# Moving the next batch's scores, transposes and values one product away from the bursts of packed weights

## The chip, the core and the metric

One NeuronCore of a Trainium2 chip runs the whole program. The metric is device time in microseconds, the median of several executions, lower is better. The matrix engine is called TensorE (PE in the profile, its weight loads PEld), the others are VectorE (DVE), ScalarE (ACT), GpSimd (POOL) and SyncE (SP), whose queue issues most of the DMA transfers.

## What is computed

The program has three parts, one behind the other. The attention and the first expert layer are where the change lies.

```python
def sm_attn(qq, kk, vv):
    s = scale * np.matmul(qq, kk.transpose(0, 1, 3, 2))
    s = s - np.max(s, axis=-1, keepdims=True)
    a = np.exp(s)
    a = a / (np.sum(a, axis=-1, keepdims=True) + 1e-09)
    return np.matmul(a, vv)
p_packed = sm_attn(p, k, v)           # p: 32 rows a head
out = sm_attn(q, p_packed, p_packed)  # batch 8, heads 8, seq 576, head_dim 64
...
h = np.maximum(np.maximum(x @ w1, x @ w2), x @ w3)   # 512 -> 768
x = h @ w_out                                        # 768 -> 512
...
h = x @ w_in                                         # 512 -> 2048
g = np.maximum(h, 0.0) + np.log1p(np.exp(-np.abs(h)))
return g @ w_out
```

## The kernel before

The work goes batch by batch through attention and the first expert layer, and the result of each batch goes to DRAM (x2d). When all eight batches are done, the softplus layer runs over all tokens (layer3 and layer4, lines 735 to 783); the change does not touch it.

For one batch, attention is packed onto the four heads' 32 rows. `transpose_kq` (185) turns a raw load of q or k into vT with a VectorE transpose (220 for q, 223 for k); four of each make a batch. There is one vT buffer: k's is given back by the first scores, and q's is given back by the second. `prep_p` (236) transposes p. `attn1_scores` (256) makes the first scores (matmuls at 247, 32 of them) into two PSUM tiles, and `attn1_exp` reduces them on VectorE (262) and exponentiates them on ScalarE (271). `attn1_transpose` (281, matmuls at 286) transposes the result, `attn1_values` (299, matmuls at 306) multiplies it by v, and `packed_transpose` (324) turns the 32 packed rows. `attn2_scores` (327), `attn2_weights` (345) and `attn2_split` (359) do the second attention, whose weights a2 have a high and a low part.

The second attention's values are never formed. Instead `packed_weights` (365) multiplies the packed rows into the weights w1, w2, w3, four column blocks at a time: 16 matmuls on 64*32 pieces of the array (line 375), here called a burst. The PSUM tile ps_w of a burst is emptied by two pairs of ScalarE and VectorE instructions one after the other, pwhi (107) then pwlo (108) for each half. `layer1_unit` (398) is one product: 12 matmuls of 128x288 (line 396), whose tile is emptied by a copy on ScalarE (419, the first of three) or a running maximum on VectorE (421, the other two). `layer1_split` and `layer2` (435) make the second product of the expert layer.

All of these PSUM tiles come from one pool `mm` of four buffers of two banks each, the whole PSUM.

The loop of lines 635 to 640 and behind runs over batches n = 1 to 7, and within one over ten slots: six slots of three layer1 products and four slots of layer2. The products are counted by u = 0 to 21: u = 3 * slot + w in the first six slots, u = 12 + slot behind. Before each product, `small_work(n, u)` (578) issues what belongs there: a burst of packed weights at u = 1, 5, 9 and 13, and, for the next batch m = n + 1, the pieces of its attention. `pinned` (569) ties each call's TensorE instructions behind those of the call before it, so that TensorE's order is exactly the written one. VectorE, ScalarE and the queues have no such order: a planner lays their instructions out in the order in which it expects them to become ready, and hands out the pool buffers in the same way. After each slot the lists `turns` and `loads` say which raw loads of q or k are transposed and issued; an entry (slot, ahead, g, which) means piece g of batch n + ahead. Raw loads have five buffers, and `narrow_ahead` (622) works the weights of the last layer from 64 to 32 bits in what is left of ScalarE and VectorE.

Of the kernel before, what the change touches and what calls it, by code (L numbers as in the profile page):

```python
# [19 lines left out]
def packed_attention_maxout_softplus(  # L20
# [155 lines left out]
    def load_p(n):  # L176
        t = tp.tile([P, NG, D], F32, tag="praw", name="praw")
        for G in range(NG):
            nc.sync.dma_start(
                out=t[:, G],  # L180
                in_=bass.AP(p.tensor, p[n, G].offset, [[NG * NP * D, NH], [D, NP], [1, D]]),
            )
        praw[n] = t
# [161 lines left out]
    def attn2_weights(n, G):  # L345
        s = s2.pop((n, G))
        sg = tp.tile([P, T], F32, tag="sg2", name="sg2")
        nc.vector.tensor_reduce(out=sg, in_=s, axis=AX.X, op=ALU.add)
        nc.vector.tensor_scalar(out=sg, in0=sg, scalar1=1e-9, scalar2=None, op0=ALU.add)
        rc = tp.tile([P, T], F32, tag="rc2", name="rc2")  # L350
        nc.vector.reciprocal(out=rc, in_=sg)
        nc.vector.tensor_tensor(
            out=s, in0=s, in1=rc.unsqueeze(2).to_broadcast([P, T, 32]), op=ALU.mult
        )
        a = sp.tile([P, S], F32, tag="s2", name="a2")
        nc.vector.transpose(out=a, in_=s.rearrange("p t n -> p (t n)"))
        a2[n, G] = a

    def attn2_split(n, G):
        hi = a2p.tile([P, S], F32R, tag="a2hi", name="a2hi")  # L360
        lo = a2p.tile([P, S], F32R, tag="a2lo", name="a2lo")
        split(a2.pop((n, G)), hi, lo)
        a2hi[n, G], a2lo[n, G] = hi, lo
# [176 lines left out]
    for name in order.split():  # L540
# [11 lines left out]
        (7, 2, 3, "k"),  # L552
    ]
    turns = [
        (1, 1, 0, "q"),
        (2, 1, 1, "q"),
        (3, 1, 2, "q"),
        (4, 1, 3, "q"),
        (9, 2, 0, "k"),
        (9, 2, 1, "k"),  # L560
# [8 lines left out]
    def pinned(fn, *args):  # L569

        if chain:
            with tc.issue_after(chain[-1]):
                fn(*args)
        else:
            fn(*args)
        chain.append(last_of(mybir.EngineType.PE))

    def small_work(n, u):


        m = n + 1
        more = m < B
        if u == 2 and more:
            pinned(prep_p, m)
            if m + 1 < B:
                load_p(m + 1)
        if u in (1, 5, 9, 13):
            pinned(packed_weights, n, (u + 3) // 4)
        if not more:
            return  # L590
        if u == 5:
            pinned(attn1_scores, m)
        elif u == 9:
            for G in range(NG):
                pinned(attn1_transpose, m, G)
        elif u == 13:
            pinned(attn1_values, m)
        elif u == 16:
            pinned(packed_transpose, m)
        elif u == 18:  # L600
            pinned(attn2_scores, m)
            pinned(packed_weights, m, 0)
        elif u == 20:
            for G in range(NG):
                attn2_weights(m, G)
        elif u == 21:
            for G in range(NG):
                attn2_split(m, G)
# [26 lines left out]
    for n in range(1, B):  # L635
        for slot in range(F1 + KC):
# [4 lines left out]
            if slot < F1:  # L641
                if slot == 1 and n + 1 < B:
                    load_v(n + 1)
                for w in range(3):
                    small_work(n, 3 * slot + w)
                    pinned(layer1_unit, n, slot, w)
            else:
                small_work(n, 2 * F1 + slot)
                pinned(layer2, n, slot - F1)
# [214 lines left out]
```

## Time and profile before

| | |
|---|---|
| median of 3 runs | 1338.73 us (1338.31 to 1339.14) |
| the profiled execution's own time | 1341.63 us |
| its span, first to last instruction | 1339.8 us |
| TensorE busy | 1304.5 us (97%) |
| VectorE busy | 894.2 us (67%) |
| ScalarE busy | 617.9 us (46%) |
| mean granted TensorE clock | 0.993 of full speed |

The profile is of one execution. A timeline lists instructions of one engine in order of time, equal neighbours merged; matmuls are pipelined, so the time of a group is best read from its start to the start of the next. The first batch that the loop touches is n = 1, from 128.6 us; n = 2 begins at 187.8, n = 3 at 247.0, n = 7 (which has no next batch) at 484.6, and the softplus layer at 536.9.

### The profile page before, as it was taken

The page shows a single profiled execution, that of the slowest core. Times are in us where ns is not written, and L with a number is a line of the kernel's source. Part 1 is how long each engine was busy: PE and PEld are TensorE (multiplying, and loading weights), DVE is VectorE, ACT ScalarE, POOL GpSimd, SP SyncE. Part 2 cuts the span into 40 slices and gives each one's busy share as a digit, 9 for nine tenths or more (in the row PEclk, how much of TensorE's full clock was granted, in tenths as well). Part 3 has the DMA queues.
Part 4 walks back from the last instruction along what each step waited for, and adds up shares of the span by engine and source line. Part 5 has one row for each costly group of instructions (what it writes and reads, how often), then busy time and mean ns, then how long its engine had stood idle before and what let it go on. Part 6 is the DMA issues. An engine that isn't in the chain of part 4 may idle for free.

```text
span 1339.8 us, 21462 instructions
## 1 busy us (share of the span) xinstructions
PE 1304.5 (97%) x8656; PEld 1100.2 (82%) x8656; DVE 894.2 (67%) x1480; ACT 617.9 (46%) x1045; POOL 0.7 (0%) x6
## 2 busy tenths in 40 slices
PE   4889999999999999999999999999999999999998
PEld 3778888898989899788888888888888888888887
DVE  4787778786878746866556566565665665655654
ACT  3544434444443435745445454454444544544443
POOL 0000000000000000000000000000000000000000
PEclk9979999999999999999999999999999999999999
DMA  9873677877577506501102011010020110000101
GB/s 269 214 197 92 170 202 180 208 212 204 178 201 201 134 36 215 159 0 38 26 1 64 0 32 32 0 47 17 4 60 0 32 32 0 24 8 1 32 1 32
DMA packets 61859, 119.17 MB, mean 89 GB/s; under 512 B 11072, under 2 KB 28736, under 8 KB 61760
## 3 DMA queue, kind: packets, MB, share of 16 engines
q1 hardware_dynamic: 55984, 106.66, 29.8%
q10 hardware_dynamic: 5776, 11.14, 2.5%
q8 instruction: 68, 1.11, 0.3%
q14 instruction: 31, 0.25, 0.1%
HBM read 90.51 MB, written 27.26 MB: 88 GB/s over the span
## 4 chain that ended last, share of the span: by engine, by line
PE 89%; DMA 5%; DVE 3%; ACT 1%; issue 1%; SPq 0%; DVEq 0%; ACTq 0%
PE ps L396 55%; PE acc L781 10%; PE acc L780 10%; PE acc L779 10%; PE ps_w L375 2%; DMA wraw<-in_moe_w_dram 1%; DMA wi_x<-wi 1%; PE ps_s L247 1%; PE ps_v L306 1%; PE ps_e L286 1%; DMA x2d<-xs 1%; DMA kraw<-in_k_dram 1%; DMA vt<-in_v_dram 1%; PE ps_k L199 1%; DVE pwlo L108 0%
## 5 line engine op out<-in xcount | busy, mean ns | idle before, releaser
L396 PE MATMUL ps<-x2hi,wilo 128*128 128x512 f32 x576 | 228.0, 396 | 0.0
L396 PE MATMUL ps<-x2lo,wihi 128*128 128x512 f32 x576 | 227.0, 394 | 0.0
L396 PE MATMUL ps<-x2hi,wihi 128*128 128x512 f32 x576 | 226.7, 394 | 0.0
L781 PE MATMUL acc<-w2hi,glo 128*128 128x512 f32 x576 | 226.0, 392 | 0.0
L780 PE MATMUL acc<-w2lo,ghi 128*128 128x512 f32 x576 | 225.7, 392 | 0.0
L779 PE MATMUL acc<-w2hi,ghi 128*128 128x512 f32 x576 | 224.5, 390 | 0.7 <-ACT ghi L107 0.7
L107 ACT ACTIVATE ghi<-t 128x512 fp32r<-128x512 f32 x144 | 91.0, 632 | 289.0 <-DVE t L761 288.6
L754 DVE TENSOR_SCALAR t<-ex 128x512 f32<-128x512 f32 x144 | 61.4, 426 | 161.9 <-ACT ex L751 161.9
L108 DVE TENSOR_TENSOR glo<-t,ghi 128x512 fp32r<-128x512 f32 x144 | 99.7, 692 | 92.6 <-ACT ghi L107 92.5
L396 PE MATMUL ps<-a2hi,pwhi 128*128 128x288 f32 x576 | 129.3, 307 | 2.5 <-ACT a2hi L107 1.3
L779 PEld LDWEIGHTS acc<-w2hi,ghi 128*128 128x128 f32 x576 | 108.2, 188 | 25.8 <-ACT ghi L107 1.2
L396 PEld LDWEIGHTS ps<-x2lo,wihi 128*128 128x128 f32 x576 | 108.1, 188 | 25.8
L396 PEld LDWEIGHTS ps<-x2hi,wilo 128*128 128x128 f32 x576 | 108.3, 188 | 25.2
L750 ACT ACTIVATE ex<-ps 128x512 f32<-128x512 f32 x144 | 86.2, 598 | 92.3 <-PE ps L396 92.2
L780 PEld LDWEIGHTS acc<-w2lo,ghi 128*128 128x128 f32 x576 | 108.1, 188 | 25.0
L396 PEld LDWEIGHTS ps<-x2hi,wihi 128*128 128x128 f32 x576 | 108.1, 188 | 24.5
L781 PEld LDWEIGHTS acc<-w2hi,glo 128*128 128x128 f32 x576 | 108.1, 188 | 23.5 <-DVE glo L108 0.4
L396 PE MATMUL ps<-a2lo,pwhi 128*128 128x288 f32 x576 | 124.3, 298 | 0.7 <-DVE a2lo L108 0.7
L396 PE MATMUL ps<-a2hi,pwlo 128*128 128x288 f32 x576 | 124.2, 297 | 0.0
L757 DVE TENSOR_TENSOR t<-ln,t 128x512 f32<-128x512 f32 x144 | 99.7, 692 | 30.4 <-ACT ln L752 30.4
L396 PEld LDWEIGHTS ps<-a2hi,pwhi 128*128 128x128 f32 x576 | 93.1, 192 | 15.8 <-ACT m L419 5.9
L761 DVE SCALAR_TENSOR_TENSOR t<-ps,t 128x512 f32<-128x512 f32 x144 | 99.5, 691 | 4.7
(90 smaller groups left out, 1847.9 us busy)
## 6 DMA issues: line engine op xcount, KB each, us to landing
qraw<-in_q_dram SPq DMA_DIRECT2D x112, 140.0 KB
kraw<-in_k_dram SPq DMA_DIRECT2D x96, 140.0 KB
wraw<-in_moe_w_dram SPq DMA_DIRECT2D x18, 512.0 KB
x2d<-xs ACTq DMA_DIRECT2D x32, 288.0 KB
x2r<-x2d SPq DMA_DIRECT2D x36, 256.0 KB
out_dram<-o SPq DMA_DIRECT2D x136, 64.0 KB
raw<-in_moe_w_in_dram SPq DMA_DIRECT2D x16, 512.0 KB
raw<-in_moe_w_out_dram SPq DMA_DIRECT2D x16, 512.0 KB
```

The source lines that it names most:

```text
L107: nc.scalar.activation(out=hi, in_=src, func=AF.Copy)
L108: nc.vector.tensor_tensor(out=lo, in0=src, in1=hi.bitcast(F32), op=ALU.subtract)
L199: nc.tensor.matmul(ps[64 * G : 64 * G + 64, i // hi, c : c + rows], r[:, i, G], ident[:rows, :rows], start=True, stop=True,)
L375: nc.tensor.matmul(ps[cols, G, : units * P].rearrange("p (w x) -> p w x", w=units), ppT[n][rows, cols], wsb[rows, 4 * c : 4 * c + units, g ...
L396: nc.tensor.matmul(o, w, xx, start=first, stop=last)
L750: nc.scalar.activation(out=ex, in_=ps, func=AF.Abs)
L754: nc.vector.tensor_scalar(out=t, in0=ex, scalar1=1.0, scalar2=-1.0, op0=ALU.add, op1=ALU.add)
L757: nc.vector.tensor_tensor(out=t, in0=ln, in1=t, op=ALU.subtract)
L761: nc.vector.scalar_tensor_tensor(out=t, in0=ps, scalar=0.0, in1=t, op0=ALU.max, op1=ALU.add)
L779: nc.tensor.matmul(ps, ghi[:, cols], whi, start=(f == 0), stop=False)
L780: nc.tensor.matmul(ps, ghi[:, cols], wlo, start=False, stop=False)
L781: nc.tensor.matmul(ps, glo[:, cols], whi, start=False, stop=(f == F2 - 1))
```

## The change

The first scores of the next batch go from u = 5 to u = 6, the transposes from u = 9 to u = 10, the values from u = 13 to u = 14. So one layer1 product stands between each of them and the burst of packed weights that they followed directly. The first three transposes of q each go one slot further down, because the single vT buffer is not free before the first scores have run.

```diff
     turns = [
-        (1, 1, 0, "q"),
-        (2, 1, 1, "q"),
-        (3, 1, 2, "q"),
+        (2, 1, 0, "q"),
+        (3, 1, 1, "q"),
+        (4, 1, 2, "q"),
         (4, 1, 3, "q"),
...
         if not more:
             return
-        if u == 5:
+        if u == 6:
             pinned(attn1_scores, m)
-        elif u == 9:
+        elif u == 10:
             for G in range(NG):
                 pinned(attn1_transpose, m, G)
-        elif u == 13:
+        elif u == 14:
             pinned(attn1_values, m)
         elif u == 16:
             pinned(packed_transpose, m)
```

## Rows read from the trace of the kernel before

**Rows 1.** The chain that ended last, by engine (section 4 of the page).

```profile
PE 89%; DMA 5%; DVE 3%; ACT 1%; issue 1%; SPq 0%; DVEq 0%; ACTq 0%
```

**Rows 2.** Busy times by stretch, batches n = 2 and n = 3.

```profile
core 0: us, PE busy (x) PEld busy (x) DVE busy (x) ACT busy (x) POOL busy (x), PEclk, DMA share, GB/s
187.80:247.00 59.20, 58.88 (x616) 53.05 (x615) 46.27 (x81) 25.04 (x44) 0.00 (x0) 1.00 0.76 196
247.00:306.40 59.40, 59.09 (x616) 53.10 (x615) 47.15 (x83) 25.00 (x44) 0.00 (x0) 1.00 0.75 201
```

**Rows 3.** Timeline of TensorE, batch n = 7: a burst alone (start us, us, engine, line, operation).

```profile
484.57 0.43 PE L396 MATMUL ps<-a2hi,pwhi 128*128 128x288 f32 x2
...
486.26 1.09 PE L375 MATMUL ps_w<-wsb,ppT 64*32 64x512 f32 x16
487.28 0.53 PE L396 MATMUL ps<-a2hi,pwhi 128*128 128x288 f32 x2
...
488.96 0.43 PE L396 MATMUL ps<-a2hi,pwhi 128*128 128x288 f32 x2
...
490.56 0.43 PE L396 MATMUL ps<-a2hi,pwhi 128*128 128x288 f32 x2
```

**Rows 4.** Timeline of TensorE, n = 2, u = 5 to 8.

```profile
197.22 1.09 PE L375 MATMUL ps_w<-wsb,ppT 64*32 64x512 f32 x16
198.10 1.18 PE L247 MATMUL ps_s<-vT,pT 64*32 64x288 f32 x32
199.21 0.53 PE L396 MATMUL ps<-a2hi,pwhi 128*128 128x288 f32 x2
...
201.24 0.51 PE L396 MATMUL ps<-a2hi,pwhi 128*128 128x288 f32 x2 [0.18 <-DVE pwlo L108]
...
203.20 0.53 PE L396 MATMUL ps<-a2hi,pwhi 128*128 128x288 f32 x2
...
204.90 0.43 PE L396 MATMUL ps<-a2hi,pwhi 128*128 128x288 f32 x2
```

**Rows 5.** Timeline of VectorE, n = 2: the second pwlo.

```profile
200.40 0.69 DVE L108 TENSOR_TENSOR pwlo<-ps_w,pwhi 128x512 fp32r<-128x512 f32 x1 [0.66 <-ACT pwhi L107]
```

**Rows 6.** Timeline of TensorE, n = 3, the first scores and the product behind.

```profile
257.30 0.68 PE L247 MATMUL ps_s<-vT,pT 64*32 64x288 f32 x12
258.29 1.16 PE L247 MATMUL ps_s<-vT,pT 64*32 64x288 f32 x20 [0.31 <-DVE vT L223]
259.38 0.53 PE L396 MATMUL ps<-a2hi,pwhi 128*128 128x288 f32 x2
```

**Rows 7.** Timeline of VectorE, n = 3: maximum of u = 4, last k transpose.

```profile
256.60 0.76 DVE L421 TENSOR_TENSOR m<-ps,m 128x576 f32<-128x576 f32 x1 [0.89 <-PE ps L396]
257.27 0.97 DVE L223 STREAM_TRANSPOSE vT<-kraw 128x576 f32<-128x576 f32 x1
```

**Rows 8.** Timeline of TensorE: half-size burst before values (n = 3), before a product (n = 7).

```profile
274.81 0.66 PE L375 MATMUL ps_w<-wsb,ppT 64*32 64x256 f32 x16
275.40 1.55 PE L306 MATMUL ps_v<-vt,e1T 96*32 96x64 f32 x96
...
509.04 0.66 PE L375 MATMUL ps_w<-wsb,ppT 64*32 64x256 f32 x16
509.63 0.53 PE L396 MATMUL ps<-a2hi,pwhi 128*128 128x288 f32 x2
```

**Rows 9.** Timeline of TensorE, first stretch: transposes of e behind a product.

```profile
64.80 0.43 PE L396 MATMUL ps<-a2hi,pwlo 128*128 128x288 f32 x2
65.07 0.82 PE L286 MATMUL ps_e<-ident,e 128*96 128x128 f32 x6
```

**Rows 10.** Timelines, n = 3: the last q transpose, the second scores.

```profile
281.57 0.77 DVE L220 STREAM_TRANSPOSE vT<-qraw 128x576 f32<-128x576 f32 x1
285.15 1.20 PE L247 MATMUL ps_s<-vT,ppT 64*32 64x288 f32 x32
```

**Rows 11.** Timeline of VectorE: first k transpose of a batch, ahead of n = 3 and n = 4.

```profile
236.24 0.97 DVE L223 STREAM_TRANSPOSE vT<-kraw 128x576 f32<-128x576 f32 x1
...
295.62 0.96 DVE L223 STREAM_TRANSPOSE vT<-kraw 128x576 f32<-128x576 f32 x1
```

## The prediction

> **What bounds the kernel now.** I read the chain of waits first. TensorE holds 89% of the chain that ended last, so the time is TensorE's, and any other engine counts only where TensorE waits for it [rows 1]. Then the busy times by stretch: the second of the batches that the change touches (n = 2) takes 59.20 us and the third (n = 3) 59.40, of which TensorE is busy 58.88 and 59.09, at the full 2.4 GHz (granted clock 1.00) [rows 2]. So there is very little idle time, and the question is what TensorE does product by product. I therefore read the timeline of TensorE and took the distance from the start of one product to the start of the next. The reader should see three things in it.
>
> A first-layer product with nothing special beside it takes 1.60 us (488.96 to 490.56). A burst of packed weights by itself costs 1.02 us, and it also lengthens its neighbours: the product before it takes 1.69 and the one behind it 1.68 [rows 3]. So entering and leaving a burst costs about 0.09 and 0.08.
>
> At u = 5 the packed weights and the first scores stand back to back. In n = 2 the burst goes over to the scores after 0.88 us and the scores to the product behind them after 1.11. But the next three products take 2.03, 1.96 and 1.70 (199.21 to 201.24, to 203.20, to 204.90). The first of these delays is put down to the second pwlo, which ends at 201.09 [rows 4, 5]. It is what gives back the PSUM buffer of the packed weights: there are four, and the two scores tiles take two at once.
>
> In n = 3 the same place looks different. The products behind are ordinary, but the scores take 2.08 us in place of 1.11, cut in two by a wait for the last transpose of k [rows 6]. That transpose starts at 257.27, right behind the maximum of u = 4, without any wait for a transfer beside it [rows 7]. So it is late by its place in VectorE's order, not by its load. The batches n = 4, 5 and 6 repeat n = 3 (scores of 2.08 each), and n = 1 repeats n = 2.
>
> **What the change takes away.** Six batches have a next one (n = 1 to 6). In n = 1 and 2 the excess is (2.03 - 1.69) + (1.96 - 1.60) + (1.70 - 1.60) = 0.80 us. With one product between burst and scores, the scores ask for their two buffers one product later, and that product, with a border on either side, takes 1.60 + 0.09 + 0.08 = 1.77 us. The product behind the scores then starts 1.02 + 1.77 + 1.11 = 3.90 us after the burst began. By then the buffer of u = 5 is free, since the maximum that empties it is 0.76 us long [rows 7] and has 1.11 us for it. In n = 3 to 6 the excess is 2.08 - 1.11 = 0.97. The scores now start at 257.30 - 0.88 + 1.02 + 1.77 = 259.2, a microsecond after the transpose of k ends (257.27 + 0.97), so that wait is gone. Sum: 2 x 0.80 + 4 x 0.97 = 5.48 us.
>
> **What it adds.** No instruction is new; what is added are the borders of the bursts.
> - Scores at u = 6: burst and scores no longer overlap (1.02 against 0.88: 0.14) and there is one more way in and out (0.09 + 0.08). 0.31.
> - Values at u = 14: one more way in and out. The half-size burst goes over to the values after 0.59 us, and to a product in the last batch after the same 0.59, so standing next to a burst saves the values nothing on their way in [rows 8]. 0.17.
> - Transposes at u = 10: in the first stretch of the kernel they follow a product at its ordinary distance (0.27 for two matmuls, 64.80 to 65.07) [rows 9], so only the way out of the burst is new, 0.08 at most, less what the transposes now lose at their own start. Between 0.03 and 0.08; I take 0.06.
>
> Together 0.54 us in each of six batches, 3.24 us.
>
> **What is moved and covered.** The q transposes (0.77 us each, two now in one slot) go to VectorE beside products. The last of them starts at 281.57 in n = 3 and the second scores, which need it, at 285.15 [rows 10]. One more in front of it leaves 3.58 - 0.77 - 0.77 = 2.04 us; without that cover, a delay would pass to TensorE one for one. The loads keep their slots on SP's queue; a raw buffer comes free up to 5 us later, far ahead of the k load that takes it. The values come 1.7 us nearer to the transpose of their result at u = 16: two products (3.3 us) are left for two short VectorE operations. I cost these at nothing. What is late next is the buffer of the packed weights at u = 6 and u = 10, by a margin of some 0.2 us or less. It costs nothing if the planner hands out the buffer of the product between, and some 0.6 us a batch at u = 6 if not (rival B).
>
> **The sum.** 5.48 - 3.24 = 2.24 us less. The profiled execution took 1341.63 us, 2.90 above the median of the runs (1338.73), so 1339.4 for it and 1336.5 for the median. Below, 0.2% (2.7 us) is about what a measurement of this kernel can tell from no change.
>
> A page speaks against part of this sum. The Trainium skill, "TensorEngine Tiling (Array Packing)", section Key Properties, says that going over to another tiling mode, not just another tile, drains TensorE. It prices no drain.
>
> **Rivals.**
> A, borders are counted by changes of shape. Packed weights and scores share 64*32, the values are 96*32, and the transposes pass as whole. Then the scores add two changes, the values one (from burst to values is one already) and the transposes none: three more of (0.09 + 0.08) / 2 = 0.085, plus 0.14. That is 0.40 us a batch, 2.4 in all, 3.1 us less: 1335.6. This is how the page's rule would count. For it: the transposes show no drain [rows 9]. Against it: the 0.59 on both sides [rows 8]. Chance 0.20.
>
> B, the PSUM wait stays. If the maximum of u = 5 is put ahead of the second pwlo and the planner hands u = 6 the packed weights' buffer, the maximum ends 1.02 + 1.77 + 0.76 = 3.55 us after the burst began, the pwlo 0.69 later, and the product goes 0.15 after that (201.09 to 201.24): 4.4 against 3.90. With the 0.10 that a broken product costs, that is 0.6 us in six batches, 3.6 less the 2.24: 1.4 us slower, 1340.1. For it: the four buffers are as full as before at that place. Against it: the buffer of u = 5 is free first. Chance 0.15.
>
> C, slower: the last transpose of k slides along with the scores. Its place on VectorE is set by the planner, and if that puts it behind the maximum of u = 5 in n = 3 to 6, it starts near 260.05 (259.2, 0.08 for the end of the product, 0.76) and ends at 261.0. The product behind the scores starts 1.14 us after it as now (258.24 to 259.38), at 262.1 against 259.2 + 1.11 = 260.3: a wait of 1.8 us in place of 0.97. Four batches lose 1.8 + 0.54 - 0.97 = 1.37 each, two gain 0.26: 5.0 us slower, 1343.7. It decides from a wait of 0.56 us (no gain left) and shows as slower from 1.23. Against it: the first k transpose of a batch stands 10.8 us ahead of the next batch's start both before n = 3 and before n = 4 (236.24, 295.62), though n = 2 had no such wait and n = 3 had [rows 11]; so the order of the k transposes is tied to the products and does not drift. Chance 0.12.
>
> That the change does not do what it says is hardly open: TensorE's order is pinned step by step. VectorE's is not, and that is C.
>
> **How the numbers follow.** My forecast (the waits go, the borders cost 0.54) has 0.53, with 1336.0 to 1337.4 as its own range; A has 0.20, B 0.15, C 0.12. The range from 1335.2 to 1340.2 takes in A and B, and leaves out C and the edges. Faster by over 0.2% means below 1336.05: A, and a twentieth from the edge of the forecast, 0.25. Slower means above 1341.4: C and a little of B, 0.14. The rest, 0.61, lies within 0.2%.
>
> **What would show it.** In the changed profile n = 2 and n = 3 should both take about 58.95 us. The scores should stand between two ordinary products with about 1.11 to the next start, without a bracket that names the k transpose; the product between burst and scores should take 1.77. The transposes of e should follow a product with no gap. A unit of 2 us behind the scores would be B, and scores of 2 us or more C. If the product between bursts takes 1.69, it is A. I am wrong altogether if a new wait stands at u = 10, 14 or 16.

## The result, and the profile after

The changed kernel took 1346.06 us (median of 4 runs, 1344.45 to 1349.45) against 1338.93 for the kernel before (4 runs): a ratio of 1.0055, with a 95% interval from 1.0042 to 1.0067. It is 7.1 us slower. I had forecast 1336.5, with at most 1340.2.

First the busy times of the changed kernel by stretch, batches n = 2 and n = 3, which answer to [rows 2].

```profile
184.10:243.35 59.25, 59.22 (x616) 52.93 (x615) 45.57 (x81) 25.16 (x44) 0.00 (x0) 1.00 0.75 192
243.35:304.33 60.98, 59.88 (x616) 53.02 (x615) 46.99 (x83) 24.86 (x44) 0.00 (x0) 1.00 0.72 196
```

Both should have taken 58.95. Batch n = 2 takes 59.25, and n = 3 takes 60.98 where it took 59.40 before. TensorE is busy for only 59.88 of it, at the full clock (1.00), so the batch contains a wait.

The timeline of TensorE in n = 2, around u = 5 and 6, answers to [rows 4] and shows the intended part of the change.

```profile
193.48 1.09 PE L375 MATMUL ps_w<-wsb,ppT 64*32 64x512 f32 x16
194.50 0.52 PE L396 MATMUL ps<-a2hi,pwhi 128*128 128x288 f32 x2
...
196.27 1.20 PE L247 MATMUL ps_s<-vT,pT 64*32 64x288 f32 x32
197.40 0.53 PE L396 MATMUL ps<-a2hi,pwhi 128*128 128x288 f32 x2
...
199.09 0.42 PE L396 MATMUL ps<-a2hi,pwhi 128*128 128x288 f32 x2
```

From start to start the burst takes 1.02, the product between 1.77 (194.50 to 196.27), the scores 1.13, and the next product 1.69. The delays of 2.03 and 1.96 behind the scores are gone. All of that is as forecast.

The same place in n = 3 on TensorE, to set beside [rows 6]:

```profile
255.52 0.70 PE L247 MATMUL ps_s<-vT,pT 64*32 64x288 f32 x12
257.30 1.16 PE L247 MATMUL ps_s<-vT,pT 64*32 64x288 f32 x20 [1.07 <-DVE vT L223]
258.39 0.53 PE L396 MATMUL ps<-a2hi,pwhi 128*128 128x288 f32 x2
```

and VectorE beside it, to set beside [rows 7]:

```profile
255.63 0.76 DVE L421 TENSOR_TENSOR m<-ps,m 128x576 f32<-128x576 f32 x1 [0.38 <-PE ps L396]
256.30 0.94 DVE L223 STREAM_TRANSPOSE vT<-kraw 128x576 f32<-128x576 f32 x1
257.13 0.65 DVE L108 TENSOR_TENSOR pwlo<-ps_w,pwhi 128x512 fp32r<-128x512 f32 x1
```

The scores now take 2.87 (255.52 to 258.39): 1.13 and a wait of 1.74 for the last transpose of k. That transpose stood behind the maximum of u = 4 before; now it stands behind the maximum of u = 5, which begins only after the scores have been issued. This is the wait that rival C describes. It repeats in n = 4, 5 and 6. By itself it costs 4 x 1.74 = 6.96 us where 4 x 0.97 had been lost before.

There is a second new wait, at u = 10. TensorE in n = 3, the product u = 9, the transposes of e, and the product u = 10:

```profile
264.38 0.53 PE L396 MATMUL ps<-a2hi,pwhi 128*128 128x288 f32 x2
...
266.06 1.47 PE L286 MATMUL ps_e<-ident,e 128*96 128x128 f32 x12
267.56 0.53 PE L396 MATMUL ps<-a2hi,pwhi 128*128 128x288 f32 x2
```

ScalarE in the same stretch:

```profile
264.85 0.58 ACT L107 ACTIVATE pwhi<-ps_w 128x512 fp32r<-128x512 f32 x1
266.37 0.60 ACT L107 ACTIVATE pwhi<-ps_w 128x512 fp32r<-128x512 f32 x1 [0.94 <-DVE pwlo L108]
266.87 0.65 ACT L419 ACTIVATE m<-ps 128x576 f32<-128x576 f32 x1
```

and VectorE:

```profile
264.14 0.77 DVE L220 STREAM_TRANSPOSE vT<-qraw 128x576 f32<-128x576 f32 x1
264.98 0.76 DVE L108 TENSOR_TENSOR hlo<-m,hhi 128x576 fp32r<-128x576 f32 x1
265.65 0.69 DVE L108 TENSOR_TENSOR pwlo<-ps_w,pwhi 128x512 fp32r<-128x512 f32 x1
```

The transposes take 1.50 to the next start instead of 1.23, which is what they take without a wait (measured below). The next product starts at 267.56, right after the ScalarE copy that empties the tile of u = 9 (266.87 and 0.65). The copy stands behind the second pwhi, this waits for the first pwlo, and that one stands on VectorE behind a transpose of q and a split. In n = 1 the transposes take 2.16, with a rebase ahead on ScalarE, and in n = 6 1.70.

**The account.** From first product to first product, the six batches take 355.93 us before and 363.31 after, 7.37 more. The terms are: the old waits, -5.48; the borders as forecast, +3.24; k's wait, +6.96; the waits at u = 10, 4 x 0.27 + 0.93 + 0.47 = +2.48. That makes 7.20. Batch n = 7 is longer too, 53.24 against 52.35. Most of that stands in one row of the page: the first product of the softplus layer waits for the last copy of layer2 (line 453) on ScalarE. Why it does so here and not before stays open:

```profile
L396 PE MATMUL ps<-x2hi,wihi 128*128 128x512 f32 x576 | 226.8, 394 | 0.7 <-ACT xs L453 0.7
```

The spans of the two profiled executions (1342.6 and 1339.8) should not be compared. The loop begins at 124.19 in one and 128.64 in the other, with the same order of work ahead of it; from 45 us up to there, the granted clock was 0.96 in the one and 0.90 in the other (means over a stretch in which it changed between its two levels, 2.4 and 1.2 GHz).

### The profile page after: what moved, and what is told of

Same layout as the page of the kernel before. It is cut to its first block, busy times and chain, and to the rows that moved or that the text cites. A ratio compares the mean times of both kernels' runs of the same rounds, so it can differ in the third digit from the quotient of the medians.

```text
span 1342.6 us, 21429 instructions
## 1 busy us (share of the span) xinstructions
PE 1303.1 (97%) x8656; PEld 1095.8 (82%) x8656; DVE 893.1 (67%) x1480; ACT 618.1 (46%) x1045; POOL 0.7 (0%) x6
## 3 DMA queue, kind: packets, MB, share of 16 engines
q8 instruction: 68, 1.11, 0.4%
## 4 chain that ended last, share of the span: by engine, by line
PE 91%; DVE 4%; DMA 2%; SPq 1%; issue 1%; ACT 1%; DVEq 0%; ACTq 0%
PE ps L396 57%; PE acc L780 10%; PE acc L781 10%; PE acc L779 10%; PE ps_w L375 2%; PE ps_s L247 1%; DMA wraw<-in_moe_w_dram 1%; PE ps_v L306 1%; DMA qraw<-in_q_dram 1%; SPq L158 1%; PE ps_e L286 1%; DVE wraw L89 0%; DMA woraw<-in_moe_w_out_dram 0%; DVE pwlo L108 0%; PE ps_k L199 0%
## 5 line engine op out<-in xcount | busy, mean ns | idle before, releaser
L396 PEld LDWEIGHTS ps<-a2hi,pwhi 128*128 128x128 f32 x576 | 91.7, 190 | 29.0 <-issue 11.4
```

What stands on the lines that cost most here:

```text
L396: nc.tensor.matmul(o, w, xx, start=first, stop=last)
```

## The experiments

Three theories, for why k's transpose moved. Theory 1: the move of the values displaces it. Theory 2: the move of the scores does (the cause that rival C names). Theory 3: the q transposes, a slot further down, do. The batches below are read from TensorE's timeline, first product to first product, in us.

```
kernel                       n=1    n=2    n=3    n=4    n=5    n=6    sum     ratio and interval
before                       59.20  59.20  59.38  59.39  59.37  59.38  355.93
after                        59.91  59.25  60.98  60.99  60.98  61.19  363.31  1.0055 [1.0042, 1.0067]
turns_only                   59.21  59.19  59.37  59.37  59.37  59.37  355.86  1.0010 [0.9999, 1.0021]
scores_only                  58.75  58.74  58.74  58.74  58.74  58.74  352.45  0.9983 [0.9973, 0.9993]
values_only                  59.39  59.37  61.13  61.12  62.65  61.13  364.78  1.0069 [1.0051, 1.0087]
transposes_only              60.21  59.51  59.73  59.71  59.71  59.71  358.57  1.0022 [1.0012, 1.0033]
after_k_pinned               59.88  59.26  59.26  59.25  59.27  59.65  356.57  0.9998 [0.9986, 1.0011]
after_v_later                60.32  59.97  60.03  59.99  60.03  59.26  359.60  1.0020 [1.0010, 1.0029]
transposes_late_half         59.25  59.25  59.43  59.43  59.43  59.43  356.23  1.0002 [0.9993, 1.0011]
after_both_mended            59.43  60.09  59.47  59.45  59.47  58.96  356.87  0.9999 [0.9990, 1.0008]
after_pinned_late_half       58.96  58.98  58.96  58.98  58.96  58.98  353.82  0.9989 [0.9977, 1.0000]
scores_before_burst          58.56  58.79  58.78  59.15  58.79  58.78  352.85  0.9982 [0.9971, 0.9992]
scores_before_burst_v_later  60.74  59.53  59.35  59.44  59.44  58.56  357.06  1.0024 [1.0011, 1.0036]
```

**turns_only**: the kernel before with the new slots of q alone.

```diff
-        (1, 1, 0, "q"),
-        (2, 1, 1, "q"),
-        (3, 1, 2, "q"),
+        (2, 1, 0, "q"),
+        (3, 1, 1, "q"),
+        (4, 1, 2, "q"),
```

> Only the q transposes go one slot down; scores, transposes of e and values stay at u = 5, 9, 13. If the values' move is what sets the last k transpose back (theory 1), nothing changes: 1338.9 us, n = 2 in 59.2 and n = 3 in 59.4, scores of 2.08 in n = 3. If it is the raw buffers of q that come free later (theory 3), the k transpose slides here as well and the scores of n = 3 take 3.5 or more: 1345.

Every batch is as before, the scores of 2.08 in n = 3 to 6 included. Theory 3 falls, and the q transposes cost nothing, as I had put it.

**scores_only**: the same turns, and the scores at u = 6; transposes and values stay.

```diff
-        if u == 5:
+        if u == 6:
             pinned(attn1_scores, m)
```

> Scores at u = 6 with the q transposes one slot down; transposes of e and values stay at u = 9 and 13. Theory 1: the last k transpose keeps its place behind the maximum of u = 4, the scores do not wait (1.13 to the next start), and a batch pays 0.31 for the new borders in place of 0.80 (n = 1, 2) or 0.97 (n = 3 to 6): 2 x 0.49 + 4 x 0.66 = 3.6 us less, 1335.3. Theory 2 (the k transposes follow the scores, since q and k share the one vT buffer): the scores of n = 3 to 6 take 2.87 as in the changed kernel: 4 x 1.08 - 2 x 0.49 = 3.3 us more, 1342.2.

The scores of n = 3 on TensorE, and VectorE's last transpose of k:

```profile
257.44 1.20 PE L247 MATMUL ps_s<-vT,pT 64*32 64x288 f32 x32
258.57 0.53 PE L396 MATMUL ps<-a2hi,pwhi 128*128 128x288 f32 x2
```

```profile
254.82 0.76 DVE L421 TENSOR_TENSOR m<-ps,m 128x576 f32<-128x576 f32 x1 [0.90 <-PE ps L396]
255.49 0.96 DVE L223 STREAM_TRANSPOSE vT<-kraw 128x576 f32<-128x576 f32 x1
```

The transpose stays behind the maximum of u = 4 (254.82) and is done a microsecond before the scores start. So the scores do not take it along: theory 2 falls. This is the part of the change that pays, 3.48 us in the batches and 1334.81 against 1337.37 in the runs. The batch has no wait at all, and the forecast's terms give it: 59.20 - 0.80 + 0.31 = 58.71 against 58.74.

**values_only**: the kernel before with the values at u = 14.

```diff
-        elif u == 13:
+        elif u == 14:
             pinned(attn1_values, m)
```

> Only the values go from u = 13 to u = 14. Theory 1: the last k transpose slides behind the first pwlo of u = 5 in n = 3 to 6, so the scores there wait some 2.6 us in place of 0.97; with 0.17 of border in six batches 4 x 1.6 + 1.0 = 7.6 us more, 1346.5. Theory 2 or 3: only the border, 1.0 us more, 1339.9.

TensorE in n = 3:

```profile
256.61 0.68 PE L247 MATMUL ps_s<-vT,pT 64*32 64x288 f32 x12
259.17 1.16 PE L247 MATMUL ps_s<-vT,pT 64*32 64x288 f32 x20 [1.88 <-DVE vT L223]
260.26 0.53 PE L396 MATMUL ps<-a2hi,pwhi 128*128 128x288 f32 x2
```

and VectorE:

```profile
255.91 0.76 DVE L421 TENSOR_TENSOR m<-ps,m 128x576 f32<-128x576 f32 x1 [0.63 <-PE ps L396]
257.55 0.69 DVE L108 TENSOR_TENSOR pwlo<-ps_w,pwhi 128x512 fp32r<-128x512 f32 x1 [0.89 <-ACT pwhi L107]
258.16 0.95 DVE L223 STREAM_TRANSPOSE vT<-kraw 128x576 f32<-128x576 f32 x1
```

The scores are where they were, at u = 5, and take 3.65: a wait of 2.54 beside 1.11. The transpose of k now stands behind a pwlo too. So the move of the values alone, which stand eight or nine products behind the scores, delays k's transpose. Theory 1 holds: the values alone are enough. Batch n = 5 has a further delay of 1.5 us behind the scores, which belongs to the clock and not to the order. The product u = 5 takes 2.80 there, and this is its stretch:

```profile
382.50:385.30 2.80, 2.80 (x14) 2.80 (x13) 1.61 (x4) 1.12 (x3) 0.00 (x0) 0.56 1.09 251
```

The granted clock is 0.56, close to TensorE's lower level of 1.2 GHz, right after TensorE had waited 2.54 for k. In n = 3, 4 and 6 it waited as long and kept 1.00, so why it fell in this one batch is not shown. Without it the sum of 8.85 us would be some 7.3.

**transposes_only**: the kernel before with the transposes of e at u = 10.

```diff
-        elif u == 9:
+        elif u == 10:
```

> Only the transposes of e go from u = 9 to u = 10. If the product behind them waits for ScalarE's copy of the product before them by the move itself, as in the changed kernel (0.28 in most batches): 0.06 + 0.28 or more in six batches, some 2 to 3 us more, 1341 to 1342, and the scores of n = 3 stay at 2.08. If that wait belongs to the other moves: 0.4 us more, 1339.3.

The wait at u = 10 is there by itself: 2.16 in n = 1 and 1.50 in the others, 2.64 us in all. It needs neither the other moves nor the new turns.

**after_k_pinned**: the changed kernel, with the maximum of u = 1 held on VectorE until the last transpose of k is issued.

```diff
-                    pinned(layer1_unit, n, slot, w)
+                    hold = k_last if 3 * slot + w == 1 else None
+                    with tc.issue_after(hold) if hold is not None else nullcontext():
+                        pinned(layer1_unit, n, slot, w)
...
+                    if which == "k" and g == NH - 1:
+                        k_last = last_of(mybir.EngineType.DVE)
```

> The changed kernel with another edit: the load of v as it was, but the maximum of u = 1 may only be issued behind the last k transpose. This sets the transpose early without touching a transfer. Place alone counts: scores of 1.13, six batches in about 356.4, ratio 1.0003. If the transfer of k lands late, the wait goes to the maximum of u = 1 and from there to a product at u = 3 to 5, which then takes 2 us or more: ratio 1.003.

VectorE at the start of n = 3, and TensorE at its scores:

```profile
247.47 1.74 DVE L223 STREAM_TRANSPOSE vT<-kraw 128x576 f32<-128x576 f32 x2
249.09 1.56 DVE L421 TENSOR_TENSOR m<-ps,m 128x576 f32<-128x576 f32 x2
```

```profile
254.16 1.20 PE L247 MATMUL ps_s<-vT,pT 64*32 64x288 f32 x32
```

The last transpose ends at 249.21, 5 us ahead of the scores, and no scores wait. With the order alone changed, the batches lose 6.74 of the 7.37 us. It also shows that the load is early enough: the transpose begins 5.9 us before the scores (248.30), where in the changed kernel it began 0.8 us after them (256.30 against 255.52), with no transfer named as what it waited for.

**after_v_later**: the changed kernel, with the load of v issued one slot later.

```diff
-                if slot == 1 and n + 1 < B:
+                if slot == 2 and n + 1 < B:
                     load_v(n + 1)
```

> The changed kernel with one edit: the load of v is issued one slot later. With it the last k transpose stands behind the first pwlo of u = 1 again, ahead of the products of u = 2 to 5. If its place is all that makes the scores wait, they go from 2.87 to 1.13 in n = 3 to 6: 4 x 1.74 = 7.0 us less than the changed kernel, six batches in 356.4 against 355.9 before the change: a ratio of 1.0003, 1337.8. If k really lands late, or the wait belongs to the scores' new place, the scores stay above 2: ratio 1.003 or more.

Not a line of k's code is touched, and the scores take 1.13 in every batch: the place of k's transposes moves with the slot in which v's load is issued. But the batches come to 359.60, not 356.4. In n = 3, VectorE behind the values (TensorE ends them at 280.2):

```profile
280.89 0.69 DVE L89 SCALAR_TENSOR_TENSOR raw<-raw 128x512 int32<-128x512 int32 x1
281.62 0.69 DVE L97 SCALAR_TENSOR_TENSOR x<-x,raw 128x512 int32<-128x512 int32 x1
282.23 0.42 DVE L86 TENSOR_SCALAR raw<-x 128x512 int32<-128x512 int32 x1
282.69 0.69 DVE L89 SCALAR_TENSOR_TENSOR raw<-raw 128x512 int32<-128x512 int32 x1
283.30 0.47 DVE L320 TENSOR_SCALAR pp<-ps_v,rc 128x64 f32<-128x64 f32 x2
```

and TensorE at the transpose of their result:

```profile
283.91 0.30 PE L231 MATMUL ps_t<-ident,pp 128*128 128x128 f32 x1 [0.24 <-DVE pp L320]
```

The short pp, which this transpose needs, is now put behind the narrowing of the last layer's weights, for which nothing waits here. The two products that I had counted as cover for it are used up. In n = 3, 4 and 5 this costs 0.49 a batch, and the transposes of e at u = 10 cost 0.27 more there than in the changed kernel (1.77 to the next start for 1.50). In n = 2 the burst behind the second scores waits as well (1.45 to its start for 0.99).

**transposes_late_half**: transposes_only, with the second half of the burst of u = 9 split only after the copy of u = 9.

```diff
-        for G in range(NG):
+        def half(G):
             split(ps[:, G, : units * P], hi[:, G, : units * P], lo[:, G, : units * P])
+        half(0)
+        if second:
+            half(1)
+        else:
+            waiting.append(half)
...
-            pinned(packed_weights, n, (u + 3) // 4)
+            pinned(packed_weights, n, (u + 3) // 4, u != 9 or not more)
...
                     pinned(layer1_unit, n, slot, w)
+                    while waiting:
+                        with tc.issue_after(last_of(mybir.EngineType.Activation)):
+                            waiting.pop()(1)
```

> Only the transposes of e at u = 10, and the second half of the burst of u = 9 is split behind the copy of the product between. If the product behind the transposes waits for that copy, which ScalarE has queued behind the second pwhi, the transposes go from 1.50 (2.16 in n = 1) to 1.22 to the next start, and the 2.6 us that the move costs come down to 0.4 to 0.5: ratio 1.0003. If 1.50 is what they cost between two products, nothing changes: 1.002.

TensorE at u = 10 in n = 3, and ScalarE's copy (a product is line 402 and the copy line 425 here):

```profile
267.67 1.47 PE L286 MATMUL ps_e<-ident,e 128*96 128x128 f32 x12
268.90 0.51 PE L402 MATMUL ps<-a2hi,pwhi 128*128 128x288 f32 x2
```

```profile
267.93 0.65 ACT L425 ACTIVATE m<-ps 128x576 f32<-128x576 f32 x1 [0.89 <-PE ps L402]
268.48 0.59 ACT L107 ACTIVATE pwhi<-ps_w 128x512 fp32r<-128x512 f32 x1
```

The copy goes ahead of the second pwhi, and the transposes take 1.23 in all six batches. So the wait at u = 10 was the buffer of the product u = 9. Without it the move of the transposes costs 0.05 us a batch (0.30 in six; I had put 0.06).

**after_both_mended**: after_v_later and this late half together.

```diff
-                if slot == 1 and n + 1 < B:
+                if slot == 2 and n + 1 < B:
...
+            pinned(packed_weights, n, (u + 3) // 4, u != 9 or not more)
```

> The changed kernel with both edits: v one slot later, and the second half of u = 9 behind the copy. What is left is the change as it was forecast: no wait at the scores, no wait behind the transposes, the borders of 0.54 a batch. Six batches in 353.7 to 354.4 (n = 1 may keep part of its wait, since a rebase of the weights stands ahead of the copy there), 1.5 to 2.2 us less than before the change: ratio 0.9984 to 0.9989, 1335.5. If the borders cost more together than alone: 355 or more.

The waits at u = 6 and u = 10 are both gone. What stays in n = 1 to 5 is what the later load of v brings (59.4 to 60.1 a batch in place of 58.95): the wait for the values' result, and in n = 2 one of 0.64 at the burst behind the second scores, for a maximum that VectorE does late. Loading v later is no mending.

**after_pinned_late_half**: the changed kernel with k pinned and the late half.

```diff
+                    hold = k_last if 3 * slot + w == 1 else None
...
+            pinned(packed_weights, n, (u + 3) // 4, u != 9 or not more)
```

> The changed kernel with the maximum of u = 1 held behind the last k transpose, the load of v where it was, and the second half of the burst of u = 9 behind the copy. If the earlier mended kernel failed to gain only because the later load of v upset the values, this one is the change as it was forecast: batches of 58.95 to 59.0, six in about 354.0 (n = 1 and 6 may differ), 1.9 us less than before the change, ratio 0.9986. If the borders themselves were priced too low, 355.5 or more.

The busy times by stretch, n = 2 and n = 3:

```profile
184.41:243.39 58.98, 58.98 (x617) 52.97 (x616) 45.44 (x81) 25.05 (x44) 0.00 (x0) 1.00 0.75 196
243.39:302.35 58.96, 58.96 (x617) 52.94 (x616) 45.62 (x80) 24.48 (x43) 0.00 (x0) 1.00 0.74 196
```

TensorE is busy for the whole of both. The batches take 58.97 in the mean, where I had forecast 58.95, and all six save 2.11 us, where I had forecast 2.24. This is the change as I had costed it; the runs give 1337.11 against 1338.24, a gain at the edge of what they resolve.

**scores_before_burst**: the kernel before, with the scores of u = 5 ahead of the burst of the same u, and k pinned. Here scores and burst stay neighbours.

```diff
+        if u == 5 and more:
+            pinned(attn1_scores, m)
         if u in (1, 5, 9, 13):
             pinned(packed_weights, n, (u + 3) // 4)
...
-        if u == 5:
-            pinned(attn1_scores, m)
-        elif u == 9:
+        if u == 9:
```

> The kernel before the change with two edits: at u = 5 the first scores go ahead of the burst instead of behind it, and the maximum of u = 1 is held behind the last k transpose. Scores and burst stay together, so no border is added, and the buffer of the packed weights is asked for again three products later, not at the next but one. If the waits at u = 5 to 8 are those of buffers and of the k transpose: all products there ordinary, batches of 58.40, six in 350.4, 5.5 us less than before: ratio 0.996. If two scores tiles and a burst fill the four buffers whatever their order: products of 2 us at u = 6 or 7, batches of 59.2.

TensorE in n = 3:

```profile
252.71 1.21 PE L247 MATMUL ps_s<-vT,pT 64*32 64x288 f32 x32
253.70 1.27 PE L375 MATMUL ps_w<-wsb,ppT 64*32 64x512 f32 x16
254.90 0.53 PE L396 MATMUL ps<-a2hi,pwhi 128*128 128x288 f32 x2
```

The waits for k and for the second pwlo are gone, but the gain is 3.08 us and not 5.5. From n = 2 on the burst takes 1.20 (1.00 in n = 1), and the two products behind it 1.78 and 1.69: with the scores' 0.99 that is 5.66 a batch where burst, scores and the same two products without waits take 0.88 + 1.11 + 1.69 + 1.60 = 5.28. Where the 0.20 in the burst comes from stays open: no row names a wait there. The rest is a new wait: the product u = 6 waits for the exponential on ScalarE (line 271), which empties a tile of the scores. It is 0.17 in the weight loads of most batches and longest in n = 4, where the product u = 5 takes 2.15 and the batch 59.15:

```profile
315.83 0.54 PE L396 MATMUL ps<-a2hi,pwhi 128*128 128x288 f32 x2 [0.30 <-ACT e L271]
```

**scores_before_burst_v_later**: the same order, without the pin and with v loaded a slot later.

```diff
+        if u == 5 and more:
+            pinned(attn1_scores, m)
...
-                if slot == 1 and n + 1 < B:
+                if slot == 2 and n + 1 < B:
```

> The same order of scores and burst at u = 5, but the k transpose comes early because the load of v is issued one slot later, with nothing held. Scores and products behind them as in the run before; the later load of v may again make the transpose of the values' result wait (0.5 to 0.7 in a batch, as it did in the changed kernel): 350.4 without it, up to 354 with it, ratio 0.996 to 0.9985.

The burst takes 1.00 here, but the later v brings a wait at u = 16 in n = 1 to 5. It is not the one for the values' result: the product behind that transpose waits, for a maximum that stands on VectorE behind the narrowing. TensorE in n = 3:

```profile
277.93 0.50 PE L396 MATMUL ps<-a2hi,pwhi 128*128 128x288 f32 x2 [0.57 <-DVE m L421]
```

The kernel is slower than before.

## Why the prediction was wrong

**What bounds the kernel, and the waits that go: right.** With its side effects mended, the change saves what the sum said (2.11 of 2.24).

**The borders: right, 0.55 against 0.54 a batch.** Scores: the burst 1.02 instead of 0.88, the product 1.77, and 0.02 more in the scores themselves, 0.33 for 0.31. Values: 0.17 for 0.17. Transposes: 0.05 for 0.06. Rival A falls at the values. At the scores it comes to the same 0.31 as the forecast, so the 1.77 of the product between decides nothing, although I had set it down as the sign. For the values it counts one change, 0.085. TensorE in n = 3 of the changed kernel, the product between, the values and the product behind:

```profile
273.14 0.53 PE L396 MATMUL ps<-a2hi,pwhi 128*128 128x288 f32 x2
...
274.92 1.55 PE L306 MATMUL ps_v<-vt,e1T 96*32 96x64 f32 x96
276.39 0.53 PE L396 MATMUL ps<-a2hi,pwhi 128*128 128x288 f32 x2
```

The product between takes 1.78 and the values 1.47 to the next start, as they did next to the burst (1.48), so the whole 0.17 is paid. The page behind that rival, the Trainium skill, "TensorEngine Tiling (Array Packing)", section Key Properties, says that changing the tiling mode drains TensorE. For the way into and out of 64*32 the trace fits that, with 0.17 around a product, without showing what the time goes into; where the transposes of 128*96 are moved away from the burst, all that is paid is 0.05.

**Rival B: did not come as such.** The product behind the scores takes 1.69. At u = 6 the buffer of the product between is in fact free. VectorE in n = 2, its maximum and the second pwlo:

```profile
196.38 0.76 DVE L421 TENSOR_TENSOR m<-ps,m 128x576 f32<-128x576 f32 x1 [0.38 <-PE ps L396]
197.05 0.68 DVE L108 TENSOR_TENSOR pwlo<-ps_w,pwhi 128x512 fp32r<-128x512 f32 x1
```

The product behind the scores starts at 197.40, when the maximum is done (197.14) and the pwlo is not (197.73).

**The step that failed first** is "so the order of the k transposes is tied to the products and does not drift". I drew it from two equal distances (10.8 us, [rows 11]) in one kernel. Such rows show that the planner repeats a pattern; they say nothing on whether another program gets the same one. And the same trace has a third distance, which I left out: ahead of n = 2 the first transpose of k stands 12.0 us ahead (175.81 against 187.84). The size of C was good (a wait of 1.74, priced at 1.8), but its chance of 0.12 was not, and neither was its cause, so that the size came out is in part luck: the scores alone leave k's transpose in its place, and the move of the values displaces it. I had costed that move by its own border and by the operations behind it, and never asked what else the planner would shift along with it.

Why the values have this reach is only partly shown. The first transpose of k for n = 3 to 6 stands 10.8 us ahead of its batch with the values at u = 13, 8.8 to 9.2 with the values at u = 14, and 11.4 to 12.0 with v's load a slot later. The turns of q, the scores and the transposes of e, moved one at a time, leave it alone. For the last transpose they do count once the values have moved: it starts 11.81 us into its batch in values_only (258.16, behind a pwlo) and 12.95 in the changed kernel (256.30, one maximum further). No run moves the others together and leaves the values. That the planner expects v late, and places the rest of the batch against that, fits both; I have argued it and not seen it. What the runs do show is that VectorE's order made the transpose late, and not its load. The Trainium skill, "Perfetto Trace Analysis", section Tensor Engine Instruction (MATMUL, LD_WEIGHTS), states that VectorE, ScalarE and GpSimd run strictly in their order; the last transpose of k, ready and yet behind a maximum that waits for TensorE, agrees with that.

**The second step that failed** is "What is late next is the buffer of the packed weights at u = 6 and u = 10, by a margin of some 0.2 us or less. It costs nothing if the planner hands out the buffer of the product between". At u = 10 it hands out that very buffer, and just this costs 0.27 to 0.93 us. I had looked only at who holds the other buffer, and not at which engine empties this one. The product u = 5 is emptied by a maximum on VectorE, which stands between the two halves of the packed weights and ahead of the second pwlo; the product u = 9 is the first of its slot, so it is emptied by a copy on ScalarE, behind the pwhi of both halves. Worth 2.48 us.

With the first failure undone the kernel is level with the one before (after_k_pinned, 0.9998); with both undone it is where the sum had put it. Together they turned 2.2 us less into 7.1 more.

**The best kernel** here is scores_only (0.9983): moving the scores alone takes away all the waits of the kernel before and pays for one pair of borders. By the runs scores_before_burst is as good (0.9982); its batches are 0.40 us longer together. The moves of transposes and values remove no wait, and cost 0.05 and 0.17 a batch even where they go well.

## What to carry to other kernels

Where a planner orders an engine's queue, a moved step can change the place of operations of which no line was touched: price not only the step but each late operation on a queue that is not pinned, and pin those that stand just ahead of a consumer. When a wait for a buffer is argued away because another buffer is handed out, look up which instruction on which engine empties that one, and what stands ahead of it there. Make the moves one at a time: of three that looked alike, one paid 3.48 us in the batches, one cost 2.64, and one cost some 7 without the fall of the clock, more than the first could bring.

## What I had not expected

The stretch ahead of the loop, of which none of these kernels edits a line, ended between 122.84 and 128.88 us in the 13 profiles, at a mean granted clock of 0.89 to 0.96 from 45 us on. That is as much as most of the effects here, while batches of the loop repeat within 0.02 us of each other (scores_only, after_pinned_late_half). For a change of a few microseconds the batches tell more than the total, and the runs' totals need many repeats.
